# The two q/k transfers of a unit: 48 rows each instead of 40

## The chip, the cores and the metric

The kernel runs on one core of a Trainium2 chip. The metric is the device time of one execution in microseconds; the time before is 279.62 us, the median of three runs (279.02 to 281.06).

## The reference

An mLSTM cell over 4 batches, 8 heads, 768 steps and head size 40, and behind it a feed-forward layer. Cut to what is computed:

```
for t in range(S):                                   # per batch and head
    m_new = max(f[t] + m, i[t]); f_s = exp(f[t] + m - m_new); i_s = exp(i[t] - m_new)
    C = f_s * C + i_s * outer(v[t], k[t]);  n = f_s * n + i_s * k[t]
    y[t] = sigmoid(o[t]) * (C @ q[t]) / max(abs(n @ q[t]), 1)
h = x @ w_in                                         # x: y as 3072 x 320
solu = h * softmax(h)
out = ((solu - mean) / sqrt(var + 1e-6) * g_ln) @ w_out
```

## The kernel before

The 768 steps of a batch are cut into six chunks of 128, and one chunk of one batch, with all its eight heads, is a unit: 24 units, the four batches of a chunk one after the other. Within a unit the recurrence is written as matrix products: scores of q and k (L1288, tile `sy`), multiplied on VectorE by the decays `d` (L1301, tile `p`), then multiplied with the values (L1355), beside the product of q with the state `C` of the chunks before (L1328) and the update of that state (L1424). The result `x` (L1382, L1396) is scaled and split into two 16-bit halves `xq`, which a DMA transpose turns into `xT` (L1489). The feed-forward layer of the unit then multiplies `xT` with `w_in` into `ph` (L1506 starts each unit's sum, L1520 goes on), forms softmax and norm on ScalarE, VectorE and GpSimd, turns the result `us` with a second DMA transpose into `big` (L1611), multiplies with `w_out` (L1666) and stores 128 rows (L1688).

The order of all work is written out by hand: the list `ORDER` names the planned operations by number, in the order in which they are issued, and each engine takes its own in that order. The planner's own search (`find`) is not used while that list stands. So a change in how long a transfer takes moves nothing in the program; it moves only when something is ready. PE gets small matmuls that compute nothing (L1704, L1708) at fixed places.

All loads, stores and DMA transposes are issued by SP, in one order, and they share 16 DMA engines. A unit's loads are `tk` (values and keys by step, 128 rows, L1144), `qk` (L1148), `gb` (the gates, broadcast to 128 rows, L1174, from the second chunk on) and, three times in the kernel, `sg` (output gates, L1189).

`qk` holds q and k with the head dimension in the partitions: even heads in rows 0 to 39, odd heads in rows 64 to 103, 4 KB a row. There are three such tiles (`QKB`), used in turn. In memory every unit's q and k are padded with zeros to 64 rows for each half. The first three units load all 128 rows, so that rows 40 to 63 and 104 to 127 of each tile are zero from then on; the 21 units behind them load the 40 rows with data of each half, in two transfers. The score products read 64 rows of a half, the product with the state (L1328) all 128.

Of the kernel before, what the change touches and what calls it, by code (L numbers as in the profile page):

```python
# [18 lines left out]
B, H, S, D = 4, 8, 768, 40  # L19
L = 128  # L20
# [27 lines left out]
QKB = 3  # L48
# [423 lines left out]
def mlstm_moe_kernel(ctx: ExitStack, tc: tile.TileContext, tok, qkT, og, fi0, fg, ig, w_in, w_out, gln, out):  # L472
# [67 lines left out]
    def g0(P, n):  # L540
        return P[G0][:, n]
# [72 lines left out]
    for j in range(2):  # L614
# [3 lines left out]
            lambda P, j=j: [  # L618
                nc.scalar.activation(
                    out=P[TG][:, j * NP + n], in_=g0(P, 3), func=AF.Copy, scale=P[DL][:, 2 * n + j : 2 * n + j + 1]  # L620
                )
                for n in range(NP)
            ],
# [495 lines left out]
    def unit(u):  # L1119
# [24 lines left out]
        load(1200, lambda P: nc.sync.dma_start(out=P[tk], in_=tok[b, c * L : (c + 1) * L, :]), [tk], prio=rank(SPQ, "tk"), behind=[("gb", u - 2)] if u > 5 else [])  # L1144

        def load_qk(P):
            for r in [slice(0, L)] if u < QKB else [slice(64 * j, 64 * j + D) for j in range(2)]:
                nc.sync.dma_start(out=P[qk][r], in_=qkT[b, c, r])  # L1148

        load(1450 if u < QKB else 1000, load_qk, [qk], prio=rank(SPQ, "qk"), behind=[("gb", u - 2)] if u > 5 else [])  # L1150
        wide = c == 0
        if wide:
# [32 lines left out]
        if u == u0:  # L1185
            for j in range(0, nu, 2):
                load(
                    1100,
                    lambda P, j=j: nc.sync.dma_start(  # L1189
                        out=P[sg][:, j : j + 2, :], in_=og[u + j : u + j + 2].rearrange("u p n -> p u n")  # L1190
                    ),
# [105 lines left out]
        for j in range(2):  # L1297
# [3 lines left out]
                lambda P, j=j: V.tensor_tensor(  # L1301
                    out=P[p_t][:, j],
                    in0=P[ps[j]].rearrange("p (n l) -> p n l", l=L),
                    in1=P[d_t][:, j],
                    op=ALU.mult,
                ),
# [380 lines left out]
        r = (b * NC + c) * L  # L1687
# [74 lines left out]
```

## Time and profile before

| | |
|---|---|
| median of three runs | 279.62 us (279.02 to 281.06) |
| the profiled execution | 282.05 us, its span 280.2 us |
| PE busy | 271.8 us, 97% of the span |
| ScalarE, VectorE, GpSimd busy | 218.2, 200.5, 167.0 us |
| DMA queue of SP | 57.33 MB, 83.5% of 16 engines' span |
| granted clock of PE | full in every slice |

The span runs from the first to the last instruction of the program; the 1.85 us between it and the execution's time lie around the program. Busy shares are averages; what an engine waits for, and when, stands in the rows below. A DMA share is the time that packets took, over 16 engines and the stretch; a packet counts whole in the stretch in which it starts, and packets that stand in each other's way count both, so it can go over 1.

### The profile page before, as it was taken

The numbers are of one execution on the slowest core, as the hardware profiler recorded it, in microseconds if no ns is written. First come the engines' busy times: TensorE is split into PE (matmuls) and PEld (weight loads), VectorE is DVE, ScalarE is ACT, GpSimd is POOL, SyncE is SP. The second block draws the span as 40 slices with busy tenths as digits, with TensorE's granted clock in tenths as the row PEclk, the third lists the DMA queues.
The fourth block names the chain that finished last, engine by engine and source line by source line (L and its number), as shares of the span: only waits on it lengthen the run. The fifth ranks groups of instructions, "written<-read, shape, count | busy, mean of one in ns | idle before, by whom it ended". The sixth has DMA issues, their size and how long they took to land.

```text
span 280.2 us, 6410 instructions
## 1 busy us (share of the span) xinstructions
PE 271.8 (97%) x2249; PEld 213.5 (76%) x2249; DVE 200.5 (72%) x460; ACT 218.2 (78%) x474; POOL 167.0 (60%) x278
## 2 busy tenths in 40 slices
PE   7999999989799999999999999999999999999995
PEld 7977987776588778778877788878787886856673
DVE  5968797799876668676956976685786966565740
ACT  4699887899949997789759659977889739665581
POOL 5026896866948588586677366576786364433411
PEclk9999999999999999999999999999999999999999
DMA  6999879679989997959999979957898994385611
GB/s 208 361 403 350 274 162 226 210 195 235 209 254 195 249 250 185 197 138 236 245 253 174 308 184 235 216 157 189 222 214 220 237 189 92 74 174 111 116 49 48
DMA packets 84852, 57.74 MB, mean 206 GB/s; under 512 B 68100, under 2 KB 75396, under 8 KB 84820
## 3 DMA queue, kind: packets, MB, share of 16 engines
q1 hardware_dynamic: 84820, 57.33, 83.5%
q8 instruction: 18, 0.29, 0.4%
q14 instruction: 14, 0.11, 0.1%
HBM read 36.41 MB, written 4.26 MB: 145 GB/s over the span
## 4 chain that ended last, share of the span: by engine, by line
PE 84%; POOL 6%; DVE 4%; issue 3%; ACT 2%; POOLq 0%; ACTq 0%; DVEq 0%
PE ph L1520 22%; PE sy L1355 9%; PE sy L1288 6%; PE ph L1704 5%; PE sy L1328 5%; PE ph L1506 2%; PE ph L1160 1%; PE so__2518 L1666 1%; PE so__2668 L1666 1%; PE so__2055 L1666 1%; PE so__2226 L1666 1%; PE so__1438 L1666 1%; PE so__3112 L1666 1%; PE so__3410 L1666 1%; PE so__3750 L1666 1%
## 5 line engine op out<-in xcount | busy, mean ns | idle before, releaser
L1666 PEld LDWEIGHTS <-big 128*128 128x128 f16 x576 | 61.4, 113 | 17.8 <-issue 0.7
L1355 PEld LDWEIGHTS sy<-tk,p 128*128 128x128 f32 x384 | 57.8, 192 | 5.2 <-issue 0.2
L1520 PE MATMUL ph<-wih,xT 128*128 128x512 f16 x192 | 58.9, 381 | 0.0
L1355 PE MATMUL sy<-tk,p 128*128 128x41 f32 x384 | 55.6, 247 | 0.1
L1216 ACT ACTIVATE d<-gb,bG 128x128 f32<-128x128 f32 x160 | 50.0, 388 | 5.5 <-POOL kt L1270 4.3
L1520 PEld LDWEIGHTS <-xT 128*128 128x128 f16 x336 | 37.3, 116 | 18.1 <-issue 1.0
L1520 PE MATMUL ph<-wil,xT 128*128 128x512 f16 x144 | 42.0, 380 | 0.0
L1301 DVE TENSOR_TENSOR p<-sy,d 128x512 f32<-128x512 f32 x48 | 32.3, 685 | 8.1 <-ACT d L1216 4.3
L1559 DVE SCALAR_TENSOR_TENSOR e<-ph,e 128x1024 f32<-128x1024 f32 x24 | 29.2, 1217 | 11.2 <-ACT e L1550 11.2
L1550 ACT ACTIVATE e<-ph,nh,hs 128x1024 f32<-128x1024 f32 x24 | 28.7, 1196 | 7.7 <-DVE nh L1543 6.9
L1468 POOL TENSOR_TENSOR xs<-x,xr 128x320 f32<-128x320 f32 x24 | 18.2, 759 | 27.0 <-DVE xr L1409 21.1
L1602 DVE SCALAR_TENSOR_TENSOR us<-e,mu,us 128x1024 f16<-128x1024 f32 x24 | 31.6, 1322 | 3.2 <-ACT us L1595 3.0
L1536 DVE TENSOR_REDUCE nm<-ph 128x1 f32<-128x1024 f32 x24 | 29.2, 1216 | 4.6 <-PE ph L1520 4.5
L1595 ACT ACTIVATE us<-e,mu 128x1024 f16<-128x1024 f32 x24 | 27.2, 1139 | 6.3 <-DVE mu L1587 6.3
L1475 POOL TENSOR_TENSOR xq<-xs,xq 128x256 f16<-128x256 f32 (+1 forms) x48 | 24.8, 538 | 8.5 <-issue 7.1
L1328 PEld LDWEIGHTS sy<-C,qk 128*128 128x128 f32 x160 | 26.6, 191 | 3.9 <-PE sy L1288 1.0
L1569 ACT ACTIVATE sq<-e,a 128x1024 bf16<-128x1024 f32 x24 | 27.3, 1138 | 1.3 <-DVE e L1559 1.3
L1396 POOL TENSOR_TENSOR x<-x,sg 128x320 f32<-128x320 f32 x24 | 20.7, 863 | 10.6 <-DVE x L1382 10.4
L1201 POOL TENSOR_SCALAR_AFFINE_SELECT gb<-gb 128x1024 f32<-128x1024 f32 x20 | 23.2, 1162 | 6.1 <-DMA gb<-gd 6.1
L1328 PE MATMUL sy<-C,qk 128*128 128x82 f32 x160 | 25.6, 259 | 0.8 <-DVE x L1382 0.8
L1288 PE MATMUL sy<-qk 64*128 64x128 f32 x384 | 26.2, 276 | 0.0
L1288 PEld LDWEIGHTS sy<-qk 64*128 64x128 f32 x384 | 24.7, 188 | 1.5 <-issue 0.5
(256 smaller groups left out, 560.6 us busy)
## 6 DMA issues: line engine op xcount, KB each, us to landing
gb<-gd SPq DMA_DIRECT2D x20, 512.0 KB
tk<-in_tok_dram SPq DMA_DIRECT2D x24, 324.0 KB
qk<-in_qkT_dram SPq DMA_DIRECT2D x42, 160.0 KB
sg<-in_og_dram SPq DMA_DIRECT2D x12, 320.0 KB
out_dram<-ot SPq DMA_DIRECT2D x24, 160.0 KB
big<-in_w_in_dram SPq DMA_DIRECT2D x5, 512.0 KB
big<-in_w_out_dram SPq DMA_DIRECT2D x4, 640.0 KB
qk<-in_qkT_dram SPq DMA_DIRECT2D x3, 512.0 KB
```

Source lines behind the costliest of these rows:

```text
L1216: nc.scalar.activation(out=P[d_t][:, j, n, :], in_=P[gb][:, h, :], func=AF.Exp, bias=P[BG][:, 0, c - 1, b * H + h : b * H + h + 1],)
L1288: nc.tensor.matmul(P[ps[j]][:, n * L : (n + 1) * L], lhsT=P[qk][r, 1, n, :], rhs=P[qk][r, 0, n, :], start=True, stop=True,)
L1301: lambda P, j=j: V.tensor_tensor(out=P[p_t][:, j], in0=P[ps[j]].rearrange("p (n l) -> p n l", l=L), in1=P[d_t][:, j], op=ALU.mult,),
L1328: nc.tensor.matmul(P[yk][:, n * 2 * E1 : (n + 1) * 2 * E1], lhsT=P[qk][:, 0, n, :], rhs=P[old][:, n, :], start=first_of_bank(), stop=False ...
L1355: nc.tensor.matmul(yv(P)[:, h, :], lhsT=P[p_t][:, j, n, :], rhs=v1(P)[:, h, :], start=first_of_bank(), stop=True, skip_group_check=True,)
L1520: nc.tensor.matmul(P[ph][:, j * 512 : (j + 1) * 512], lhsT=P[xT][:, a, :], rhs=P[w][:, k, j * 512 : (j + 1) * 512], start=False, stop=n == 6,)
L1536: lambda P: V.tensor_reduce(out=P[nm], in_=P[ph], axis=AX.X, op=ALU.max, negate=True),
L1550: lambda P: nc.scalar.activation(out=P[e], in_=P[ph], func=AF.Exp, bias=P[nh], scale=P[hs], accum_out=P[z]),
L1559: lambda P: V.scalar_tensor_tensor(out=P[e], in0=P[ph], scalar=2.0**-15, in1=P[e], op0=ALU.mult, op1=ALU.mult, accum_out=P[a]),
L1569: lambda P: nc.scalar.activation(out=P[sq], in_=P[e], func=AF.Square, bias=P[a], scale=-float(DFF), accum_out=P[su]),
L1602: lambda P: V.scalar_tensor_tensor(out=P[us][:, 1], in0=P[e], scalar=P[mu], in1=P[us][:, 0], op0=ALU.add, op1=ALU.subtract),
L1666: nc.tensor.matmul(P[po][:, 0:DM], lhsT=uTv(P, a)[:, k, :], rhs=P[w][:, k, :], start=n == 0, stop=n == 23)
```

## The change

The two transfers of a unit take rows 0 to 47 and 64 to 111 instead of 0 to 39 and 64 to 103: the 40 rows with data of each half and the 8 rows of zeros behind them, which stand in memory beside the data. The first three units, which load 128 rows in one transfer, stay. No instruction of any engine moves; what changes is the size of 42 transfers, from 40 rows (160 KB) to 48 rows (192 KB).

```diff
         def load_qk(P):
-            for r in [slice(0, L)] if u < QKB else [slice(64 * j, 64 * j + D) for j in range(2)]:
+            for r in [slice(0, L)] if u < QKB else [slice(64 * j, 64 * j + 48) for j in range(2)]:
                 nc.sync.dma_start(out=P[qk][r], in_=qkT[b, c, r])
```

## Rows read from the trace of the kernel before

**Rows 1.** The page: busy engines, clock by slice, the DMA queues.
```profile
PE 271.8 (97%) x2249; PEld 213.5 (76%) x2249; DVE 200.5 (72%) x460; ACT 218.2 (78%) x474; POOL 167.0 (60%) x278
...
PEclk9999999999999999999999999999999999999999
...
q1 hardware_dynamic: 84820, 57.33, 83.5%
q8 instruction: 18, 0.29, 0.4%
```

**Rows 2.** Busy time by stretch; the last three numbers: PE clock, DMA share, GB/s.
```profile
core 0: us, PE busy (x) PEld busy (x) DVE busy (x) ACT busy (x) POOL busy (x), PEclk, DMA share, GB/s
35.00:45.00 10.00, 9.91 (x91) 8.01 (x88) 7.84 (x21) 8.80 (x24) 9.20 (x12) 1.00 0.76 201
45.00:57.00 12.00, 11.18 (x101) 9.32 (x100) 9.78 (x26) 9.49 (x27) 8.93 (x13) 1.00 0.85 208
57.00:62.00 5.00, 4.20 (x33) 3.48 (x32) 4.68 (x11) 5.00 (x13) 3.90 (x7) 1.00 0.75 165
62.00:70.00 8.00, 7.94 (x67) 5.47 (x66) 7.85 (x17) 7.58 (x21) 4.21 (x6) 1.00 1.02 237
70.00:77.00 7.00, 5.12 (x47) 3.87 (x44) 5.85 (x15) 7.00 (x18) 6.61 (x12) 1.00 1.14 206
77.00:100.00 23.00, 23.00 (x196) 18.63 (x195) 15.49 (x37) 19.07 (x39) 14.68 (x25) 1.00 0.99 235
100.00:150.00 50.00, 50.00 (x420) 39.77 (x419) 36.34 (x85) 39.99 (x96) 35.00 (x57) 1.00 0.90 208
150.00:200.00 50.00, 50.00 (x431) 39.98 (x429) 36.87 (x84) 39.75 (x87) 32.73 (x53) 1.00 0.88 211
200.00:240.00 40.00, 40.00 (x335) 30.39 (x334) 30.19 (x71) 31.92 (x75) 24.08 (x43) 1.00 0.87 188
```

**Rows 3.** Waits of PE and of its weight loads: total us, times, longest us.
```profile
PE ph L1506 <- DVE nh L1543: 1.9, 1, 1.9
...
PE so__707 L1424 <- POOL kt L1270: 0.8, 1, 0.8
PE sy L1328 <- DVE x L1382: 0.8, 1, 0.8
...
PEld L1506 <- DMA xT<-xq: 2.1, 1, 2.1
```

**Rows 4.** PE in order of time, 73 to 77 us: start, us, what.
```profile
73.85 0.31 PE L1666 MATMUL so__980<-woh,big 128*128 128x320 f16 x1
76.04 0.39 PE L1506 MATMUL ph<-wih,xT 64*128 64x512 f16 x1 [1.88 <-DVE nh L1543]
```

**Rows 5.** SP in order of time, 60 to 80 us.
```profile
66.06 0.84 SPq L1148 DMA_DIRECT2D qk<-in_qkT_dram  x2
67.00 0.55 SPq L1174 DMA_DIRECT2D gb<-gd  x1
67.60 0.59 SPq L1189 DMA_DIRECT2D sg<-in_og_dram  x1
68.91 1.24 SPq L1489 DMA_TRANSPOSE xT<-xq  x1
70.20 0.58 SPq L1144 DMA_DIRECT2D tk<-in_tok_dram  x1
...
77.25 1.21 SPq L1489 DMA_TRANSPOSE xT<-xq  x1
...
79.18 0.42 SPq L1144 DMA_DIRECT2D tk<-in_tok_dram  x1
```

**Rows 6.** DMA issues by line, and the durations (min/median/max ns) of L1148's.
```profile
qk<-in_qkT_dram SPq DMA_DIRECT2D x42, 160.0 KB
L1148 SPq DMA_DIRECT2D qk<-in_qkT_dram x45: 282/350/725, 9.5 to 211.5; - x45
```

**Rows 7.** Busy time by stretch again: the first loads, and two stretches of q/k rows.
```profile
2.00:14.00 12.00, 12.00 (x93) 11.84 (x93) 10.50 (x22) 6.55 (x18) 2.74 (x10) 1.00 0.95 329
67.66:68.12 0.46, 0.46 (x5) 0.24 (x3) 0.46 (x2) 0.23 (x1) 0.46 (x2) 1.00 0.66 255
213.60:214.60 1.00, 1.00 (x10) 0.86 (x9) 0.00 (x0) 1.00 (x5) 1.00 (x2) 1.00 0.64 164
```

**Rows 8.** The page: the span (the execution's 282.05 us stand in the table above).
```profile
span 280.2 us, 6410 instructions
```

**Rows 9.** GpSimd in order of time, 40 to 50 us.
```profile
46.93 1.09 POOL L1201 TENSOR_SCALAR_AFFINE_SELECT gb<-gb 128x1024 f32<-128x1024 f32 x1 [2.65 <-DMA gb<-gd]
```

**Rows 10.** SP in order of time, 40 to 41 us.
```profile
40.04 0.60 SPq L1174 DMA_DIRECT2D gb<-gd  x1
40.74 0.87 SPq L1148 DMA_DIRECT2D qk<-in_qkT_dram  x2
```

**Rows 11.** Waits of SP's DMA queue: total us, times, longest us.
```profile
SPq L1489 <- ACT xq L1462: 16.3, 11, 3.8
```

**Rows 12.** SP in order of time, 77 to 220 us: first and last q/k issues (14 pairs).
```profile
84.00 0.88 SPq L1148 DMA_DIRECT2D qk<-in_qkT_dram  x2
...
209.75 2.08 SPq L1148 DMA_DIRECT2D qk<-in_qkT_dram  x4
```

## The prediction
> **What bounds the kernel now.** I read the page first, for what is busy: TensorE (PE) works 271.8 of 280.2 us at the full clock, in all 40 slices, while the DMA engines are busy for 83.5% of their time [rows 1]. So two things could set the end, and the table by stage tells them apart. From 77 to 240 us PE is busy for the whole of every stretch (23.00 of 23, 50.00 of 50, twice, 40.00 of 40), although the DMA share there is 0.87 to 0.99; before that it has holes, in five stretches 10 - 9.91 + 12 - 11.18 + 5 - 4.20 + 8 - 7.94 + 7 - 5.12 = 3.65 us [rows 2]. The list of PE's waits names them: 0.8 us for `kt`, 0.8 us for `x`, and 1.9 us in front of L1506. The last is printed as a wait for VectorE's `nh`, but the weight load of the same line, for which PE has to wait too, waited 2.1 us for the transfer of `xT`, and `nh` is no operand of a matmul; so it was the transfer [rows 3]. No row of these lists has PE waiting for q or k. The reader is to see that q/k transfers matter only by what stands behind them in the DMA queue, and only ahead of 77 us.
>
> The hole of 1.9 us ends at 76.04, when the matmul of L1506 starts [rows 4]. Its `xT` was issued by SP (SyncE) at 68.91 and was in PE's hands only 7.1 us later. The same transfer issued at 77.25 is nowhere among PE's waits. What stood ahead of it is in SP's order: two q/k transfers at 66.06, `gb` at 67.00, `sg` at 67.60 [rows 5]; the DMA share of 62 to 70 and of 70 to 77 us is 1.02 and 1.14, which means packets queued on nearly every engine [rows 2].
>
> **The change part by part.** No row moves on any engine: the same 42 issues stand at the same places, each with 48 rows of 4 KB in place of 40, 192 KB for 160 KB [rows 6]. 42 x 32 KB = 1.38 MB more are read, 2.4% of the queue's 57.33 MB [rows 1].
>
> How many engines carry 40 rows can be read where q/k rows move almost alone. From 67.66 to 68.12 us, behind the end of a `big` transpose, the share is 0.66: 0.66 x 16 = 10.6 engines at 255 GB/s, 24 GB/s each. From 213.60 to 214.60 us, behind four q/k issues in a row, it is 0.64: 10.2 engines, but 164 GB/s, 40 rows of 4 KB in one microsecond [rows 7]. So a 40-row transfer works on ten engines with four rows each, and takes 160 KB / 255 GB/s = 0.64 us undisturbed and 1.0 us when several follow each other; a row then holds its engine 0.25 us. While loads of 128 rows run at the start the share is 0.95 at 329 GB/s, so sixteen engines can work [rows 7].
>
> [...]
>
> Cost of one 48-row transfer, from both sides. Best: sixteen engines at the 24 GB/s each that the ten reach in the short stretch, 196.6 KB / 384 GB/s = 0.51 us, half a microsecond less than the 1.0 us of the queued case. Worst: the 164 GB/s are a limit that more engines do not lift, 196.6 KB / 164 GB/s = 1.20 us, 0.2 us more. I take three rows on each of sixteen engines (48 / 16) at 0.25 us, 0.75 us: the row of 213.60 shows ten engines fully busy and six not, which is what a limit in the engines looks like. That is 0.25 us less per transfer, 0.5 us per unit; the ends are -1.0 and +0.4 us per unit.
>
> [...]
>
> Sum, step by step, on the profiled execution (span 280.2, in all 282.05 us [rows 8]):
> - `xT` of 68.91 has one unit's q/k pair of the same backlog ahead: 0.5 us earlier, and PE's 1.9 us become 1.4. -0.5 us.
> - The holes for `kt` and `x` (0.8 us each) come after GpSimd's wait of 2.65 us for `gb` at 46.93 [rows 9]. That `gb` was issued at 40.04, ahead of the pair of 40.74 [rows 10], so it has no q/k of its own backlog ahead: 0, and at best -0.25 us for rows that shared its engines.
> - 77 to 240 us: what lands earlier there is hidden under PE, which never stops [rows 2]: 0. Without that cover it would be 0.5 us for each of the 14 pairs issued there, the first at 84.00 us, the last at 209.75 among four issues [rows 12]: 7 us.
> - SP's issues: 350 ns median now [rows 6], against 0.42 to 0.58 us for the 128-row `tk` [rows 5]. Eight rows of the 88 between them cost at most (0.58 - 0.35) x 8 / 88 = 0.02 us, 0.9 us over 42; SP itself waits longer than that for operands (16.3 us at the `xT` issues alone [rows 11]): 0.
> - The rows of zeros write what already stands there; PE reads the same 64 rows: 0.
>
> That gives 281.55 against 282.05 us. The median of the runs is 279.62 (279.02 to 281.06), 2.43 us under the profiled execution, so part of the 3.65 us of holes is not there in an ordinary run. I carry over 0.3 of the 0.5 us: **279.3 us**.
>
> **The rivals.**
> 1. The transfer is no shorter, or the same: rows are paced by something that extra engines don't lift (or 48 rows go to twelve engines with four each). For it: 164 GB/s with ten busy engines, when the same ten do 255 for a while. Against it: 329 GB/s at the start. Price 0 to +0.4 us on `xT` of 68.91, and the hole grows to 2.3: 279.6 to 280.0 us.
> 2. Slower: the extra rows lengthen the queue and transposes start to come late after 77 us too. The place is the `xT` in front of L1506, the price up to 0.4 us per unit. It decides when a transfer takes over 1.0 us and the lead of `xT` over its matmul is used up; `xT` issued at 77.25 landed before its use, and PE waits for no transfer from 77 to 240 us, which speaks against it. If each of the 14 pairs behind 77 us cost 0.4 us: 5.6 us, 285.2 us.
> 3. Faster by much: balance lets all transfers behind q/k come early, and every hole closes. 282.05 - 3.65 = 278.4 us, which is only 0.4% under the median. For it: the backlog of 62 to 77 us; against it: `kt` and `x` have other waits behind them. Past 278.4 there is nothing to take, since PE's order and clock stay.
> 4. Chance: 18 instruction packets of together 0.29 MB take 0.4% of 16 engines' span [rows 1], 0.004 x 16 x 280.2 / 18 = 1.0 us each on one engine. If one of them meets a transpose or `gb`, the last engine lands 1 us late. A small shift may make or end such a meeting: +/-1 us, 278.6 to 280.6 us, in either kernel.
>
> **How the numbers follow.** The forecast has 0.5, rival 1 0.25, rival 2 0.05, rival 3 0.1, and a shift of rival 4 as the main effect 0.1. A change of under about 1% (2.8 us) is one that this measurement can hardly tell from none. Faster than 276.8 us would need more than all of PE's holes: 0.03. Slower than 282.4 us needs rival 2, or rival 1 and 4 together: 0.05. The rest, 0.92, is no change. The range reaches from rival 3 with a little less around the span, 278.1, to rival 1 with 4 on top, 281.0.
>
> **What would show it.** In the changed profile a stretch with q/k rows alone should have a share near 1.0 and over 200 GB/s (rival 1: 164 GB/s or less, or a share of 0.75); 42 issues of 192 KB; PE's wait in front of L1506 near 76 us below 1.9 us; PE full from 77 to 240 us. A wait of PE for `xT` or `big` after 77 us, once per unit, would prove me wrong by rival 2; a median under 277 us would mean that PE's own pace changed, which I hold for excluded.

## The result, and the profile of the changed kernel

The changed kernel takes 281.06 us (median of 19 runs, 278.86 to 284.40) against 279.51 us for the kernel before in the same series (277.46 to 281.06): a ratio of 1.0059 with a 95% interval of 1.0032 to 1.0086. So it is about 1.6 us slower. Every ratio here is to the kernel before on the same chip and leaves executions out that were over 1.5% above their kernel's fastest, so it is not always that of the medians. The forecast was 279.3 us, a little faster; the time lies just above the range (281.0) and inside the case "within 1%".

The profiled execution of the changed kernel took 282.39 us. Its page, with the lines that answer to [rows 1, 8]: the span, busy engines, clock by slice, and DMA queues as packets, MB and share of 16 engines' span.

```profile
span 280.7 us, 6410 instructions
...
PE 274.3 (98%) x2249; PEld 215.4 (77%) x2249; DVE 199.7 (71%) x460; ACT 218.4 (78%) x474; POOL 165.9 (59%) x278
...
PEclk9999999899999999999999999999999999999999
...
q1 hardware_dynamic: 85408, 58.71, 88.5%
q8 instruction: 18, 0.29, 0.4%
```

The instructions are the same 6410 and the bytes are the expected 1.38 MB more (58.71 for 57.33). But the DMA engines' time, share times span, went from 0.835 x 280.2 = 234.0 to 0.885 x 280.7 = 248.4 us: 6% more time for 2.4% more bytes. By the forecast's three rows of 0.25 us on sixteen engines, 12 engine-us for 10, it would have been 42 x 2 / 16 = 5.3 us more; it is 14.4. One slice of the clock is not full; more on that below.

The table by stage of the changed kernel, with the stretches of [rows 2] (the last three numbers: PE clock, DMA share, GB/s):

```profile
35.00:45.00 10.00, 9.91 (x96) 8.07 (x92) 7.77 (x21) 8.81 (x23) 9.60 (x12) 1.00 0.89 222
45.00:57.00 12.00, 11.95 (x82) 9.60 (x81) 9.15 (x24) 9.70 (x29) 8.74 (x13) 0.86 1.06 210
57.00:62.00 5.00, 4.88 (x47) 4.06 (x45) 4.55 (x12) 4.79 (x12) 4.08 (x7) 1.00 0.88 256
62.00:70.00 8.00, 8.00 (x63) 5.70 (x61) 7.85 (x19) 7.38 (x18) 5.01 (x8) 1.00 0.98 212
70.00:77.00 7.00, 6.43 (x60) 5.09 (x60) 6.30 (x16) 6.95 (x20) 4.55 (x10) 1.00 1.20 201
77.00:100.00 23.00, 22.40 (x191) 18.03 (x190) 15.48 (x37) 19.69 (x40) 14.46 (x24) 1.00 1.08 249
100.00:150.00 50.00, 50.00 (x419) 39.76 (x418) 36.20 (x85) 40.10 (x95) 35.01 (x57) 1.00 0.93 213
```

PE's waits and its weight loads' waits in the changed kernel (total us, times, longest us), to be held against [rows 3]:

```profile
PE so__1301 L1666 <- DMA big<-us: 0.6, 1, 0.6
PE ph L1506 <- DVE rd L1373: 0.6, 1, 0.6
...
PEld L1506 <- DMA xT<-xq: 1.5, 3, 0.8
...
PEld L1666 <- DMA big<-us: 0.9, 1, 0.9
```

Two things stand here. The hole of 1.9 us in front of L1506, on which the forecast had put its whole gain, is 0.6 us, so that "below 1.9 us" came true, though not by a shorter transfer, as the next profiles show. And there is a new wait after 77 us, 0.6 us for `big` at 91 us, where the forecast saw PE full. Yet summed over the rows PE has *fewer* holes than in the profile of before, while the kernel is slower. This pair of profiles cannot carry the comparison, and the reason turned out to be a reading of its own.

**What one profile is worth here.** A second profile of either kernel was taken (labels b40 and a48). The kernel before, profiled again, has a span of 276.7 us; between 14 and 100 us its only wait is this one:

```profile
PE so__1301 L1666 <- DMA big<-us: 0.2, 1, 0.2
```

The holes for `xT`, `kt` and `x` of [rows 3] are not there. The table puts the span of several profiles beside PE's busy time from 14 to 240 us (226 us long) and beside the time lost to a lower granted clock (the busy part of a stretch times one less its clock):

| kernel profiled | span | holes of PE 14 to 240 us | lost to the clock | span less both |
|---|---|---|---|---|
| before, first | 280.2 | 3.65 | 0 | 276.6 |
| before, again | 276.7 | 0.39 | 0 | 276.3 |
| changed, first | 280.7 | 1.58 | 1.7 | 277.4 |
| changed, again | 279.0 | 2.11 | 0 | 276.9 |
| 64 rows | 283.1 | 6.03 | 0 | 277.1 |
| 48 rows ahead of 77 us, first | 283.2 | 3.50 | 3.1 | 276.6 |
| 48 rows behind 77 us | 281.3 | 2.76 | 1.7 | 276.8 |
| 128 rows ahead of 77 us, again | 276.8 | 0.48 | 0 | 276.3 |

Busy times of that stretch, for the kernel before profiled again and for the changed kernel profiled again, one after the other:

```profile
14.00:240.00 226.00, 225.61 (x1914) 178.85 (x1914) 170.50 (x404) 189.70 (x423) 152.18 (x236) 1.00 0.92 221
```

```profile
14.00:240.00 226.00, 223.89 (x1899) 177.06 (x1898) 170.80 (x403) 188.52 (x423) 151.55 (x236) 1.00 0.98 226
```

Over eighteen profiles worked out in this way (the first of 42 rows and that of rows 40 to 87, below, are not among them) the last column lies between 275.4 and 277.4, 276.5 in the mean. So the kernel is a floor of 276.5 us of span, 278.4 us of time with the 1.85 us around it, plus the holes of that execution; 278.4 us was rival 3's figure for "every hole closes". Which hole opens varies between executions as much as the kernels differ. By their medians the kernel before stands 1.1 us above the floor, the changed one 2.7.

The hole in front of L1506 at 74 to 76 us, on which the forecast stood, opens in three of these profiles: 1.9 us in the first of before, 2.4 us with 48 rows ahead of 77 us, and 2.5 us with 48 rows behind 77 us, where every load up to that place is that of before. PE's wait in the last of them:

```profile
PE ph L1506 <- DMA xT<-xq: 2.5, 1, 2.5
```

So 40 rows have it as well as 48. In the first two the trace's list of packets shows what goes with it. In the first profile of before an instruction packet of 16 KB holds one DMA engine from 73.96 to 74.90 us; fifteen of the sixteen landing signals of `xT` come by 74.49, the last at 75.99. With 48 rows ahead of 77 us it is a packet at 73.76 and a last signal at 76.00, the others by 74.51. When the kernel before was profiled again, the packet came at 72.34, behind all sixteen signals (71.95 to 72.05), and there is no hole. In the third profile all sixteen signals are late, 75.12 to 75.22, and why stays open.

### The profile page after: what moved, and what is told of

Read it like the earlier page. It is cut to its first block, busy times and chain, and to the rows that moved or that the text cites. A ratio compares the mean times of both kernels' runs of the same rounds, so it can differ in the third digit from the quotient of the medians.

```text
span 280.7 us, 6410 instructions
## 1 busy us (share of the span) xinstructions
PE 274.3 (98%) x2249; PEld 215.4 (77%) x2249; DVE 199.7 (71%) x460; ACT 218.4 (78%) x474; POOL 165.9 (59%) x278
## 3 DMA queue, kind: packets, MB, share of 16 engines
q1 hardware_dynamic: 85408, 58.71, 88.5%
## 4 chain that ended last, share of the span: by engine, by line
PE 80%; DMA 8%; DVE 6%; POOL 2%; issue 1%; ACT 1%; POOLq 0%; ACTq 0%; DVEq 0%
PE ph L1520 20%; PE sy L1355 9%; PE sy L1288 7%; PE ph L1704 6%; PE sy L1328 4%; DMA xT<-xq 4%; DMA big<-us 3%; PE ph L1506 2%; DMA sg<-in_og_dram 1%; PE ph L1160 1%; DVE us L1602 1%; PE so__1301 L1666 1%; DVE wol L1067 1%; PE so__2518 L1666 1%; PE so__2668 L1666 1%
## 5 line engine op out<-in xcount | busy, mean ns | idle before, releaser
L1288 PE MATMUL sy<-qk 64*128 64x128 f32 x384 | 27.4, 281 | 0.0
L1288 PEld LDWEIGHTS sy<-qk 64*128 64x128 f32 x384 | 25.7, 192 | 1.8 <-issue 0.7
```

Of the source, the lines that this page charges most:

```text
L1288: nc.tensor.matmul(P[ps[j]][:, n * L : (n + 1) * L], lhsT=P[qk][r, 1, n, :], rhs=P[qk][r, 0, n, :], start=True, stop=True,)
```

## The experiments

All kernels are the kernel before with one line changed, the list of row ranges in `load_qk`; `D` is 40, `L` is 128.

### The pace of a transfer: 42, 48 and 64 rows

```diff
-            for r in [slice(0, L)] if u < QKB else [slice(64 * j, 64 * j + D) for j in range(2)]:
+            for r in [slice(0, L)] if u < QKB else [slice(64 * j, 64 * j + 42) for j in range(2)]:
```

and the same with 64.

> The two q/k transfers of a unit take 42 rows each (2 of zeros): 14 engines with three rows each would work instead of 10 with four, and only 5% more bytes move. In the changed kernel four transfers of 48 rows in a row landed about 1.2 us apart, four of 40 rows 1.0 us apart, 25 ns for each row. If a transfer into one half of the partitions is paced by its rows (25 ns each), 42 rows take 1.05 us and the time is that of before plus at most 0.4 us. If more engines by themselves do the harm (they get in the way of the transposes), it is slower by about 1 us, like the change. If the engines were the limit, it is 0.3 us faster or the same.

> The two q/k transfers of a unit take 64 rows each: 16 engines with four rows. If rows pace a transfer at 25 ns, one takes 1.6 us, 0.6 us more than with 40, a unit 1.2 us more, and the kernel loses 2.4 times what the change lost or more: 283 us and up, with waits of PE for xT and big at several places. [...]

> 42 rows again, for a profile at the full clock. Four q/k transfers in a row should land about 1.05 us apart if each row costs 25 ns, and 0.75 us apart if 14 engines with three rows each set the pace. If what hurts is that a transfer lies on the engine that also fetches instructions, and that is one of the last two, PE has no wait for big at 91 us here; if it is any other or if lateness alone counts, 0 to 0.8 us.

Measured: 42 rows 279.88 us, ratio 0.9988 (0.9954 to 1.0022); a second run, taken for its profile, 279.65 us. 64 rows 286.71 us, 1.0195 (1.0108 to 1.0281), from four executions. The pace is read where [rows 7] read it, behind the four q/k issues in a row near 210 us (busy time by stretch; the last two numbers are the DMA share and GB/s). The changed kernel, 48 rows:

```profile
213.00:216.00 3.00, 3.00 (x26) 2.08 (x23) 1.37 (x4) 3.00 (x10) 1.97 (x4) 1.00 1.06 163
```

42 rows, the third of the four, from its first row to the first row of the next:

```profile
211.52:212.61 1.09, 1.09 (x10) 0.76 (x9) 0.24 (x2) 1.09 (x4) 0.94 (x2) 1.00 0.92 162
```

64 rows, likewise:

```profile
216.73:217.93 1.20, 1.20 (x10) 0.74 (x9) 0.61 (x2) 1.20 (x6) 0.68 (x1) 1.00 1.07 222
```

The share next to last says that sixteen engines work at 48 rows (1.06 of 16), as the forecast had it, where ten did at 40 (0.64). But the GB/s stay at 163, where ten engines made 164. With 42 rows they are 162 at a share of 0.92, near fourteen engines. A 48-row transfer in such a row therefore takes 196.6 KB / 163 GB/s = 1.21 us, not 0.75; one of 42 rows takes 1.09, of 64 rows 1.20, of 40 rows 1.0 us as before. From 40 to 48 rows that is 25 ns for each row, as the expectations had it for rows that set the pace; 64 rows take no longer than 48. So what was expected of 64 rows held for the kernel (283 us and up, 286.71 measured) and failed on the transfer (1.6 us, 1.20 measured). Sixteen engines are now held for 1.2 us where ten were for 1.0, which goes with the 88.5% of the queue.

This is the pace behind other q/k rows. The first transfer of a run, right behind a transpose, is fast in every kernel with two transfers a unit: in the changed one, the first of the four and then the second:

```profile
212.35:212.90 0.55, 0.55 (x14) 0.55 (x12) 0.55 (x1) 0.55 (x3) 0.55 (x1) 1.00 1.18 348
212.90:214.11 1.21, 1.21 (x15) 1.00 (x14) 0.48 (x2) 1.21 (x6) 1.10 (x3) 1.00 1.05 163
```

And 19 of the 21 pairs stand alone. Taken from the trace's packets, at the eight or nine such places from 40 to 200 us where no rows of the gates (4 KB too) stand beside them, a pair lasts, from the start of its first row to the end of its last, 2.26 and 2.35 us in the mean with 40 rows (two profiles), 2.35 and 2.42 with 48, 2.96 with 64. So for most pairs 48 rows are longer by some 0.1 us, no more than two profiles of one kernel differ, and not by twice the 0.21.

PE's waits with 64 rows show what a longer transfer does:

```profile
PE ph L1506 <- DMA xT<-xq: 3.2, 4, 1.5
PE so__1301 L1666 <- DMA big<-us: 1.6, 1, 1.6
...
PE sy L1288 <- DMA qk<-in_qkT_dram: 0.5, 1, 0.5
PE so__980 L1666 <- DMA big<-us: 0.5, 1, 0.5
```

These are the transposes that stand behind q/k in the queue, and once the q/k rows themselves.

### One transfer of 128 or 112 rows in place of two

```diff
-            for r in [slice(0, L)] if u < QKB else [slice(64 * j, 64 * j + D) for j in range(2)]:
+            for r in [slice(0, L)]:
```

and with `slice(0, 112)` for the 21 units.

> q/k of every unit come in one transfer of 128 rows (all rows, zeros included), 512 KB instead of twice 160 KB. If the limit is that a transfer reaches only half of the partitions, both halves at once take 512 KB at some 390 GB/s = 1.3 us instead of twice 1.0, and all behind them in the queue comes 0.7 us earlier per unit: 0.5 to 1.5 us faster than before, although 8.06 MB more are read. If bytes are what counts (the reads, the engines' time), 352 KB more... that is 192 KB more per unit than before, three times what the change added (64 KB), and it is slower than the change: over 282 us.

> q/k of a unit come in one transfer of rows 0 to 111, 448 KB: 16 engines with seven rows. As for one transfer of 128 rows, with 1.15 us in place of 1.3: 0.1 to 0.3 us faster than that one if the transfer's length counts; if bytes count, slower than the change, 281.5 us and up.

(The bytes added by 128 rows are 4.13 MB, 61.46 less 57.33, not the 8.06 of the expectation.) Measured: 128 rows 280.16 us, 1.0004 (0.9968 to 1.0040); 112 rows 280.22 us, 1.0025 (0.9992 to 1.0057). The same stretch with 128 rows:

```profile
211.40:213.40 2.00, 2.00 (x25) 1.70 (x22) 0.53 (x2) 2.00 (x9) 1.73 (x3) 1.00 1.03 399
```

A share of 1.03 again, but 399 GB/s: 524 KB, both halves together, in 1.31 us, where two of 40 rows behind each other take 2.0 and two of 48 take 2.4 us; where it stands alone, its mean is 2.29 us, as long as a pair of 40. As many bytes as with 64 rows (61.46 MB), 21 issues fewer, and no slower. So it is not the bytes that cost, and not that sixteen engines share the work.

What then orders the times? Not the pair's own length alone: lone pairs of 48 rows are hardly longer than those of 40. The time for which the DMA engines are held does it better, share times span of the queue, in us per engine:

| rows per transfer | MB | engines held, us | time against before, us |
|---|---|---|---|
| 40, two profiles | 57.33 | 234.0, 236.0 | 0 |
| 42 | 57.67 | 237.2 | -0.3 (-1.3 to +0.6) |
| 128, one transfer | 61.46 | 241.0 | +0.1 (-0.9 to +1.1) |
| 112, one transfer | 60.08 | 243.0 | +0.7 (-0.2 to +1.6) |
| 48, two profiles | 58.71 | 248.4, 249.1 | +1.6 (+0.9 to +2.4) |
| 64 | 61.46 | 258.5 | +5.5 (+3.0 to +7.9) |

(The last column is the ratio's distance from one times 279.6 us.) With 128 and with 64 rows the same bytes move, at 241 and at 258 us of the engines. The queue's time rises first without any effect, and then the holes come: 64 rows keep the engines busy for 91.3% of the span. This is an order that goes along with the times, not a proof: packets that stand in each other's way lengthen the sum too (the share is 1.20 from 70 to 77 us in the changed kernel).

### The same 48 rows on other partitions

```diff
-            for r in [slice(0, L)] if u < QKB else [slice(64 * j, 64 * j + D) for j in range(2)]:
+            for r in [slice(0, L)] if u < QKB else [slice(40, 88) for j in range(2)]:
```

> Both transfers of a unit go to rows 40 to 87 (24 rows in either half of the partitions) instead of rows 0 to 47 and 64 to 111: as many transfers, rows, bytes and engines as in the changed kernel, only other partitions; q and k of most heads stay those of an older unit, so this kernel is for the pace of the transfers alone. Theory P (a transfer is paced by the part of the partitions that it reaches): where q/k rows move alone behind the four issues near 210 us they take 0.6 to 0.9 us each (220 to 330 GB/s) instead of 1.2 us, and the loss ahead of 77 us goes. Rival E (192 KB on sixteen engines take 1.2 us wherever they land): 1.2 us and 163 GB/s as in the changed kernel. [...]

The second transfer of a unit overwrites the rows of the first, so SP waits until that one has landed; the four issues near 245 us take 7.18 us of SP for 2.23, and the kernel's 322.25 us say nothing about the pace. But two transfers, the second of one unit and the first of the next, follow each other freely, and nothing else moves there:

```profile
250.25:251.00 0.75, 0.75 (x5) 0.34 (x4) 0.72 (x3) 0.68 (x3) 0.00 (x0) 1.00 0.96 366
249.75:251.25 1.50, 1.50 (x9) 0.78 (x8) 1.45 (x4) 1.43 (x3) 0.00 (x0) 1.00 0.84 262
```

In the full stretch they move at 366 GB/s, 196.6 KB / 366 = 0.54 us each; with the start and the end, 1.6 us for the two, and the second lands 0.58 us behind the first. That is not to be held against the 1.21 us of four in a row, since these two come into an empty queue. In the changed kernel the pairs issued at 117.37 and 188.11 us come into a nearly empty one, their first rows 1.2 and 1.0 us behind the issue: they take 2.0 and 1.9 us, and the second lands 0.9 us behind the first. The number of rows, bytes and engines is the same; rows 40 to 87 lie in both halves of the partitions, rows 0 to 47 in one. So theory P (a transfer is paced by the partitions that it reaches) has the direction for it, with 0.58 for 0.9 us, and rival E, 1.2 us wherever they land, is out. Two things stay open: the rows read from memory are others as well, and no run has four such transfers in a row.

### Which pairs cost

48 rows in some units only, 40 in the others: units 3 to 9 (the seven pairs issued ahead of 77 us, twice), units from 10 on, units 3 and 4, units 5 to 9, all but 3 and 4; and 64 rows in units 5 to 9.

```diff
-            for r in [slice(0, L)] if u < QKB else [slice(64 * j, 64 * j + D) for j in range(2)]:
+            for r in [slice(0, L)] if u < QKB else [slice(64 * j, 64 * j + (48 if u < 10 else D)) for j in range(2)]:
```

The others have another condition in the place of `u < 10`: `u >= 10`, `u < 5`, `5 <= u < 10`, `u >= 5`.

> 48 rows only for the seven units whose q/k are issued ahead of 77 us (units 3 to 9), 40 rows for the 14 behind. If the change loses its time where PE has holes (each pair 0.4 us longer, so xT and gb come later ahead of 77 us), this one is as slow as the change, +0.5 to +0.6%, and late48 is like before. If the wait for big at 91 us is the loss, it is like before: -0.2 to +0.2%.

> 40 rows for the seven units whose q/k are issued ahead of 77 us, 48 rows for the 14 behind, the first of them at 84 us. If the wait of PE for big at 91 us (0.6 to 0.8 us in the changed kernel, none before) is a consequence of the 48 rows of the pair issued just ahead of it, it is seen here too and the time is +0.3 to +0.6%. If the loss lies ahead of 77 us, it is like before: -0.2 to +0.2%.

> 48 rows only in units 3 and 4, whose pairs are issued at 21 to 31 us; all others 40. Theory D1 (the loss comes from the first backlog, in front of xT of 36 us and the gates behind it): most of what 48 rows in units 3 to 9 cost (0.48%), so 0.3 to 0.5% slower. Rival D2 (it adds up over all seven units ahead of 77 us): 2/7 of that, 0.1%, not to be told from none.

> 48 rows only in units 5 to 9, 40 in all others. Units 3 to 9 together cost 0.48%, units 3 and 4 alone nothing measurable, units from 10 on 0.11%. Theory M (the loss is made by the pairs of units 5 to 9, issued at 37 to 77 us among gates, transposes and output gates): 0.4 to 0.5% slower. Rival S (the loss is a sum of small delays over all of them): 0.2 to 0.3%.

> 64 rows only in units 5 to 9, 40 in all others. 64 rows in all units cost 1.95%. Theory M (place): most of that, 1.2 to 1.7% slower, with PE's holes between 35 and 92 us at 4 us or more. Rival L (a longer pair costs wherever it is issued, and the many pairs after 77 us make most of it): 5 of 21 units, 0.3 to 0.6%.

> 48 rows in units 3 to 9 a second time. It came out 0.48% slower, while its two parts, units 3 and 4 alone and units 5 to 9 alone, came out at 0.00% and 0.07%. Theory I (the delays add up in the queue, and cost only when more than the slack ahead of an xT is used up; both parts are needed): again 0.3 to 0.6% slower. Rival A (the first figure was too high and parts add): 0.0 to 0.2%.

> 48 rows in all units but 3 and 4. The changed kernel (all units) is 0.59% slower. Theory I (units 3 and 4 are needed for the loss, since the backlog of 20 to 40 us starts with them): 0.1 to 0.2%, not to be told from none. Rival A (parts add: 0.07% of units 5 to 9 and 0.11% of units from 10 on): 0.2%. Rival T (the loss does not depend on where the pairs are, only on how many): 19 of 21 units, 0.5%.

| rows | units | pairs | ratio | 95% interval |
|---|---|---|---|---|
| 48 | all (the change) | 21 | 1.0059 | 1.0032 to 1.0086 |
| 48 | from 5 on | 19 | 1.0044 | 1.0010 to 1.0079 |
| 48 | from 10 on | 14 | 1.0011 | 0.9973 to 1.0048 |
| 48 | 3 to 9 | 7 | 1.0048, again 1.0018 | 1.0020 to 1.0076, again 0.9984 to 1.0051 |
| 48 | 5 to 9 | 5 | 1.0007 | 0.9988 to 1.0026 |
| 48 | 3 and 4 | 2 | 1.0000 | 0.9963 to 1.0037 |
| 64 | all | 21 | 1.0195 | 1.0108 to 1.0281 |
| 64 | 5 to 9 | 5 | 1.0026 | 0.9998 to 1.0053 |

After the first two rows of results I held that the loss is made ahead of 77 us, by units 5 to 9 (theory M); mid48 and mid64 struck that down. Then I held that the delays of units 3 and 4 are needed, and those of 5 to 9 on top of them (theory I); from5, slower by 0.44% without units 3 and 4, spoke against that, though its interval begins at 0.10%, and early48 came out lower the second time. What is left is the plain reading that fits the intervals: the loss goes with the number of longer pairs, and no small group of them makes it. The intervals are too wide to say more: whether the parts add, or cost only where enough of them come together, as 64 rows against 48 would suggest, stays open. The time for which the engines are held, the order of the table further up, fits these kernels too: 237.0 us (units 5 to 9), 237.9 (3 and 4), 241.9 (from 10 on), 241.6 and 244.1 (3 to 9), 242.2 (64 rows in 5 to 9), 243.9 (from 5 on), 248.4 and 249.1 (all).

### The mirror image: one transfer in some units

128 rows in one transfer, but only in units below 10, twice; and in all units but 10 and 11, whose pairs stand ahead of the wait for `big` at 88 to 91 us.

```diff
-            for r in [slice(0, L)] if u < QKB else [slice(64 * j, 64 * j + D) for j in range(2)]:
+            for r in [slice(0, L)] if u < 10 else [slice(64 * j, 64 * j + D) for j in range(2)]:
```

> Units 3 to 9 load all 128 rows of q/k in one transfer, the 14 units from 10 on their two transfers of 40 rows as in the kernel before. Theory D (what costs is the time for which a q/k transfer holds up what is queued behind it ahead of 77 us; a pair of 40 rows takes 2.0 us, one transfer of 128 rows 1.3 us in the runs so far): 0.7 us less per unit ahead of 77 us, the mirror image of 48 rows, so up to 1.4 us faster, 278.1 to 279.2 us, ratio 0.995 to 0.999, and fewer waits for xT there. Rival B (bytes moved ahead of 77 us): 7 x 192 KB more, slower than 48 rows in the same units, ratio over 1.01. Rival N (the holes ahead of 77 us have other causes in the kernel before): ratio 1.000.

> 128 rows in one transfer for units 3 to 9, 40-row pairs from unit 10 on, a second time, since the first left it open whether this beats the kernel before (ratio 0.997, interval 0.994 to 1.000). Theory D (a shorter hold of the queue ahead of 77 us is worth part of PE's holes there): again 0.2 to 0.5% faster. Rival: 1.000.

> All units load 128 rows in one transfer but units 10 and 11, the pairs ahead of the wait for big at 88 to 91 us, which load two transfers of 40. With 128 rows in every unit the time was that of the kernel before, and PE waited 1.2 us for big there. Theory W (that wait ate what the shorter transfers gave): it goes, and the kernel is 0.3 to 0.5% faster than before, 278.1 to 278.7 us. Rival (the wait comes from the place of the instruction packet, not from these two loads): it stays at about 1 us, ratio 1.000.

Measured: early128 278.93 us, 0.9970 (0.9940 to 1.0000), and again 278.68 us, 0.9974 (0.9945 to 1.0003). Taken together, with the half widths as errors, that is 0.9972 with a half width of 0.0021: about 0.8 us faster than the kernel before, as theory D had it, though small. The engines are not held for less here (85.6% of 277.6 and 85.8% of 276.8 us, 237.6 and 237.5), so that order does not explain it; nor is the shorter transfer of theory D shown as its reason, since one of 128 rows that stands alone is as long as a pair of 40 (2.29 us). Why it is faster stays open. The 128 rows everywhere had shown no gain; their profile has a wait for `big` of 1.2 us near 91 us. With units 10 and 11 at 40 rows that wait is down to 0.2 us,

```profile
PE so__1293 L1666 <- DMA big<-us: 0.2, 1, 0.2
```

and the span near the floor, 276.7 us; but the ratio, 0.9985 (0.9957 to 1.0013), can't be told from one, so theory W has the profile for it and not the time. That wait also shows where units 10 and 11 have 40 rows (0.9 us in the profile of first48), so these two pairs are not its only cause.

### Second looks

> The kernel before once more, unchanged, for a second profile of it. In the first one PE lost 1.9 us in front of L1506 at 74 to 76 us, when an instruction packet of 16 KB held one engine and the last of sixteen parts of xT came 1.5 us behind the others; and it had no wait for big at 91 us. If that meeting belongs to one execution only, the hole at 74 us is 0.3 to 0.6 us here and the span is under 279 us; if it comes each time, the hole is again 1.5 to 2 us.

> The changed kernel again, for a second profile. If the loss is the later xT and gates ahead of 77 us: PE waits 2 to 4 us in all for transfers ahead of 92 us, where the second profile of the kernel before has 0.2 us, and PE is busy without a hole from 92 to 240 us. If it is the granted clock alone: a stretch at 0.5 with no wait ahead of it.

Their spans stand in the table of the first section. The changed kernel again (280.78 us) has a full clock in every slice, a wait of 1.2 us for `big` at 91 us, 0.4 for `x` and 0.3 for `xT`. Two profiles of the changed kernel thus have 0.6 and 1.2 us for `big`, two of the kernel before 0 and 0.2: the wait that comes nearest to being the change's own. The kernel with 48 rows from unit 10 on, which has the longer pair just ahead of it, does not show it, though.

## Why the prediction was wrong, point by point

**What bounds the kernel** was read rightly: PE from 77 us on, and the DMA queue ahead of it. What was read too much into was the list of holes: the 1.9 us in front of L1506 is a property of that execution and not of the kernel: it goes with an instruction packet that met `xT`, and the second profile of before has nothing of it. The text saw the warning itself (the median lies 2.43 us under the profiled execution), scaled the gain down for it, but kept the hole as the only place where the change could act.

**No instruction moves, 42 issues of 192 KB, sixteen engines.** Right: 6410 instructions as before, share 1.06 in a stretch of q/k rows.

**Cost of a 48-row transfer: this step failed.** It was taken at "three rows on each of sixteen engines (48 / 16) at 0.25 us, 0.75 us", and measured 1.21 us in a row; lone pairs of 48 rows came out some 0.1 us longer in the mean, and not 0.5 shorter. The premise was that the ten busy and six idle engines at 213.60 look like a limit in the engines. It was not one: with sixteen engines on the same half each row holds its engine longer, 163 GB/s on sixteen engines are 10 GB/s each, or 4 KB in 0.40 us, for 0.25 us before. That 48 rows take sixteen engines, three rows each, was my estimate, which no row of before shows; the run bore it out (a share of 1.06, and in the list of packets three rounds of sixteen rows to a transfer), but with 0.40 us for a row. The worst case of the text, 1.20 us with the 164 GB/s as a limit that more engines do not lift, was exact for transfers in a row, and rival 1's sign, 164 GB/s or less, was seen. The 255 GB/s read as "undisturbed" belong to the first transfer behind a transpose, and that one is fast with 48 rows too (348 GB/s).

**The `xT` hole, -0.5 us:** failed with it; and the hole was not made by the q/k pair but goes with an instruction packet. That it was 0.6 us in the changed kernel's first profile is luck. **77 to 240 us, 0:** failed in part. PE was busy 22.40 of 23 us from 77 to 100 in the changed kernel, 21.80 when profiled again, for 23.00 and 22.82 before. Behind 100 us it holds: 139.84 of 140 us. **`kt`, `x`, zeros:** nothing that the rows can tell from before.

**SP's issues, +0.02 us each:** too low. All durations of L1148 in the changed kernel (min/median/max ns), beside [rows 6]:

```profile
L1148 SPq DMA_DIRECT2D qk<-in_qkT_dram x45: 326/420/1074, 9.6 to 211.9; - x45
```

The median grew by 70 ns. SP's queue had room for it, as the text said: with its issues in order (start, us), it stands still from 70.72 to 72.08 us.

```profile
68.86 1.24 SPq L1489 DMA_TRANSPOSE xT<-xq  x1
70.15 0.57 SPq L1144 DMA_DIRECT2D tk<-in_tok_dram  x1
72.08 5.22 SPq L1611 DMA_TRANSPOSE big<-us  x1
```

**The rivals.** Rival 1 happened, but with a larger price: 0 to +0.4 us were put on one `xT`, and 1.6 us came. The engines are held for 14 us longer over the whole kernel (248.4 for 234.0), and what of that reaches the end comes through holes that differ between executions; pricing one place of one profile could not give that. How the longer hold becomes 1.6 us is not shown step by step. Rival 2 (5.6 us, once per unit behind 77 us) did not happen with 48 rows. With 64 rows it begins to: PE was busy 138.16 of the 140 us from 100 to 240 us. Rival 3 gave the floor rightly; the kernel that comes near it (early128, 278.7 and 278.9 us) does so without shorter q/k transfers where they stand alone. Rival 4, a packet of instructions that makes one engine late, is what the hole of 1.9 us shows; no run moved such a packet on purpose.

The range missed by 0.06 us because its upper end was rival 1 at one place plus one meeting.

## What to carry to other kernels

Price a DMA transfer by the partitions that it reaches before counting engines or bytes: here one transfer over all 128 partitions took 1.31 us where two of 40 rows, one into each half, took 2.0 us. That is for transfers behind each other; alone in the queue the one lasted 2.29 us and the two 2.26 and 2.35. Where a nearly full queue feeds the bound engine, the time for which loads hold the DMA engines went along with the loss here (234 to 258 us held, none to 5.5 us lost), also where no row shows the bound engine waiting for that load. And a hole in one profile is a sample: profile the kernel a second time before a forecast rests on one hole, and price a delay of every unit as a sum over all units with a share that reaches the end.

## What the runs showed of the hardware

**More engines, the same rate up to 48 rows.** Into one half of the partitions, behind other q/k rows, ten engines moved 164 GB/s (40 rows, a share of 0.64), about fourteen 162 (42 rows, 0.92), sixteen 163 (48 rows, 1.06) and 222 (64 rows, 1.07); over both halves sixteen moved 399 (128 rows, 1.03). The first transfer of a run was faster, 348 GB/s with 48 rows. One transfer of 128 rows took 1.31 us where two of 40 took 2.0, but lone transfers lasted as long as lone pairs (2.29 us for 2.26 and 2.35), and the kernel with 128 rows everywhere was no faster (1.0004).

**The granted clock fell in some executions.** In the first profile of the changed kernel PE worked for 3.5 us at a granted clock of 0.51, though it had been busy without a hole ahead of it:

```profile
42.00:48.00 6.00, 6.00 (x42) 4.50 (x39) 4.29 (x15) 4.93 (x13) 3.56 (x5) 1.00 1.16 186
48.40:51.90 3.50, 3.50 (x24) 2.88 (x25) 2.27 (x8) 2.74 (x9) 3.42 (x6) 0.51 1.07 314
```

With 48 rows ahead of 77 us it fell behind a hole of 2.4 us for `xT`, and stayed at 0.50 for the 6 us behind it:

```profile
74.00:75.00 1.00, 0.00 (x0) 0.00 (x0) 0.89 (x5) 1.00 (x2) 1.00 (x4) 1.00 1.00 286
...
76.00:82.00 6.00, 5.96 (x22) 3.81 (x23) 0.94 (x4) 2.02 (x5) 0.00 (x0) 0.50 0.88 209
```

So two of the holes came with a second loss: 2.4 us of waiting and 3.1 us of clock here, and 2.5 and 1.7 us with 48 rows behind 77 us, while the hole of 1.9 us of [rows 3] and the 6.03 us of smaller holes with 64 rows cost no clock. Why it fell in the first profile of the changed kernel, without a hole, is open.
